# Token sums by matrix multiply, or by VectorE's block transposes: the RMS root of a fused attention and gated-MLP kernel

## The chip, the cores and the metric

One NeuronCore of a Trainium2 chip runs the whole program. The metric is the device time of one launch in microseconds (us), the median of several runs. A profile of one execution of the kernel before gives the span from the first to the last instruction and every instruction's start and length.

## The reference

Windowed attention over 8 batches, 8 heads, 576 positions of 64 numbers (four heads see the last 32 positions, four heads every fourth of the last 128) makes x, 4608 tokens of 512 numbers. Then comes a gated MLP with an RMS norm in front:

```python
rms = np.sqrt(np.mean(x * x, axis=-1, keepdims=True) + 1e-06)
xn = x / rms * rms_g
g = xn @ w_gate                               # 512 -> 1536
silu = g * (1.0 / (1.0 + np.exp(-g)))
out = (silu * (xn @ w_val)) @ w_out           # 1536 -> 512
```

Everything is float32. What matters here is the row `rms`: for each token, a sum of 512 squares, and then its inverse root multiplied into all 512 numbers.

## The kernel before

**Tiling.** The tokens are cut into 16 units of 288 (`u` = 0 to 15, half a batch each). Inside a unit the features lie on the 128 partitions in four blocks (`c` = 0 to 3), and the 288 tokens are the columns. The MLP's 1536 inner features are 12 blocks of 128 (`j` = 0 to 11). From u = 1 on, a float32 product is made of three matmuls on rounded parts (high by high, high by low, low by high), written `hi` and `lo` in names.

**Ticks.** The program is one list of ticks written out in advance. For each j of a unit there are three: `gate` (12 matmuls into `g`), `val` (12 into `v`) and `proj` of the j before (12 into the four `acc` banks). So a unit's MLP has 36 ticks. The attention of unit u + 1 is threaded between them: one burst at a time makes scores `s`, transposes `t` and outputs `o`. I number a unit's norm by the ticks of the MLP of the unit before it: tick 28 is a `val`, 29 a `proj`, 30 a `gate`, 31 a `val`, and tick 36 is the first `gate` that reads the normed x.

**Order in a tick.** `later(dt, rank, fn)` puts a piece of work off by dt ticks. `flush` issues a tick's pieces sorted by rank, ahead of the tick's matmuls. Each engine runs what it is given in that order and never lets a later instruction pass an earlier one that waits. Ranks that matter: the row sums and scaling of attention (`scores_norm`) -1, `prod` and `tanh` 0, the split of h into high part (ScalarE, `hhi`) and low part (GpSimd, `hlo`) 0.5, `silu` 0.6, `scores_max` 0.7, the low part of q (`q_lo`) 0.9 in tick 29.

**PSUM.** There are eight banks and each tag has one. `g` of block j and `v` of block j + 1 share a bank, `v` of j and `g` of j + 1 the other one. In a `val` tick in which attention also transposes, the tile `t` is taken new from the bank of that j's `g` (`bank("g", j)`), so its first write comes after the last reader of that `g`, which is `silu` (L724). Tick 31 is such a tick in the norms of u = 3 to 14; u = 15 has no next unit and so no attention then.

**The norm before**, for u = 1 to 15. `square` (ScalarE) squares each block of x and the squares are added into `xsq`, the last addition on VectorE in tick 28. `rms_sum` ends tick 28 with three matmuls of float32 (six in the trace) that sum over the partitions. `rms_root` in tick 29: VectorE adds the epsilon (L593), GpSimd raises [96, 3] numbers to the power -0.5 (L594), splits them (L599, L600); VectorE and ScalarE put both parts on diagonals (L608, L612). `rms_apply` ends tick 30 with two matmuls against ones (L628), which leave the root of every token on all partitions in the PSUM tile `bps`. `normal` (L642) multiplies x by it in ticks 31, 32, 32 and 33, and `part` splits the result for the MLP of tick 36 on.

Of the kernel before, what the change touches and what calls it, by code (L numbers as in the profile page):

```python
# [77 lines left out]
def attn_moe(ctx: ExitStack, tc: tile.TileContext, qk_in, v_in, w_gate, w_val, w_out, rms_g, outT):  # L78
# [16 lines left out]
    A.copy(out=ones, in_=one.to_broadcast([P, P]))  # L95
    inv = cst.tile([P, 2], F32, name="inv")
    G.memset(inv, 1.0 / DM)
    mhalf = cst.tile([QB, U // QB], F32, name="mhalf")
    G.memset(mhalf, -0.5)
    mask = cst.tile([QB, P], F32, name="mask")  # L100
    G.memset(mask, 0.0)
# [18 lines left out]
    def later(dt, rank, fn):  # L120
        put_off.setdefault(now[0] + dt, []).append((rank, fn))
# [299 lines left out]
    def take(u, c, i, o, heads_of=(0, 1)):  # L421

        blocks, nq, _ = geometry(u, c)
        if (u, c) not in xraw:
            xraw[u, c] = sb.tile([P, U], F32, tag="xraw", name=f"xraw_{u}_{c}", bufs=NC)
        x = xraw[u, c]
        if c < NC // 2:
            to = x[:, QB * i:QB * i + nq]
        else:
            to = x.rearrange("p (j r) -> p r j", r=DIL)[:, i, :]  # L430
        if u == 0:
            A.copy(out=to, in_=o[:, :nq])
        elif u < NEX:
            for a in range(2):
                A.copy(out=to[a * D:(a + 1) * D], in_=o[a * D:(a + 1) * D, a * nq:(a + 1) * nq])
        else:
            for a in heads_of:
                ours, cols = to[a * D:(a + 1) * D], 2 * a * nq
                V.tensor_reduce(out=ours, in_=o[:D, cols:cols + 2 * nq].rearrange("d (t q) -> d q t", t=2),  # L439
                                axis=mybir.AxisListType.X, op=ALU.add)  # L440
                V.tensor_tensor(out=ours, in0=o[D:, cols:cols + nq], in1=ours, op=ALU.add)  # L441
        if i == len(blocks) - 1 and 1 in heads_of:
            if u == 0 and c == NC - 1:
                square(u, c)
                return
            dt = 1 if c != 1 or u < NEX else 4
            later(dt, 0.44 if u >= NEX and (now[0] + dt - ends) % 3 == 0 else 2.5 if u else 1.9, lambda: square(u, c))

    def square(u, c):
        first = c == 0  # L450
        sq = sb.tile([P, U], F32, tag="xsq" if first else "tmp", name=f"sq_{u}_{c}", bufs=1 if first else 2)
        x = xraw[u, c]
        A.activation(out=sq, in_=x, func=AF.Square)
        if u == 0:
            if c < NC - 1:
                G.tensor_scalar(out=x, in0=x, scalar1=gs[:, c:c + 1], scalar2=1.0, op0=ALU.mult, op1=ALU.mult)
            else:
                A.activation(out=x, in_=x, func=AF.Copy, scale=gs[:, c:c + 1])
        if u == 0:
            squares.append(sq)  # L460
        elif first:
            xsq[u] = sq
        else:
            later(1, 0.4, lambda: (V if c == NC - 1 or u == 1 else G).tensor_tensor(out=xsq[u], in0=xsq[u], in1=sq, op=ALU.add))

    def bursts(u):
        return [(u, c, i) for c in range(NC) for i in range(len(geometry(u, c)[0]))]
# [16 lines left out]
    def products(q, t, o, t_ps, s_tag="s", o_tag="o", wait=0):  # L484
# [50 lines left out]
        if o:  # L535
            if o[0] < NEX or wait:
                later(1, 0.41 if o[0] < NEX else 0.55, lambda: take(*o, o_ps))
            else:
                for a in range(2):
                    later(1, (0.1, 0.3)[a], lambda a=a: take(*o, o_ps, (a,)))  # L540
            if o[0] < NEX:
                later(1, 9, lambda: load_v(further(o, 3)))
            far = further(o, 2)
            if far and far[0] >= NEX:
                split_v(far, 8 if o[0] < NEX else 1)
# [30 lines left out]
    def rms_sum(u):  # L576
        if u == 0:
            part_sum(NC - 1)
            later(1, -1.2, lambda: rms_root(u, sum_ps))
            later(1, 0.75, spread_first)  # L580
            return
        r_ps = ps.tile([QB, NB, 2], F32, tag="o", name=f"rps_{u}")
        for i in range(NB):
            PE.matmul(r_ps[:, i, :], xsq[u][:, i * QB:(i + 1) * QB], inv, start=True, stop=True)
        later(1, 0.1 if u == 1 else -1.2, lambda: rms_root(u, r_ps))

    def rms_root(u, r_ps):
        r = sb.tile([QB, NB], F32, tag="rst", name=f"rst_{u}", bufs=2)
        total = r_ps[:, :, 0]
        if u == 0:  # L590
            V.tensor_reduce(out=r, in_=r_ps[..., 0].rearrange("q c i -> q i c"), axis=mybir.AxisListType.X, op=ALU.add)
            total = r
        V.tensor_scalar(out=r, in0=total, scalar1=1e-6, scalar2=None, op0=ALU.add)  # L593
        G.tensor_tensor(out=r, in0=r, in1=mhalf, op=ALU.pow)  # L594
        if u == 0:
            rst[u] = [r]
            return
        r_hi, r_lo = (sb.tile([QB, NB], F32R, tag=f"rst_{p}", name=f"rst_{p}_{u}", bufs=1) for p in ("hi", "lo"))
        G.tensor_copy(out=r_hi, in_=r)  # L599
        G.tensor_tensor(out=r_lo, in0=r, in1=r_hi, op=ALU.subtract)  # L600
        rst[u] = []

        def spread():
            for p in (r_hi, r_lo):
                d = sb.tile([QB, NB, QB], F32R, tag="tmp", name=f"rd_{u}_{len(rst[u])}", bufs=2)
                rst[u].append(d)
                if p is r_hi:
                    V.tensor_tensor(out=d, in0=ident[:QB, None, :QB].to_broadcast([QB, NB, QB]),  # L608
                                    in1=p[:, :, None].bitcast(F32).to_broadcast([QB, NB, QB]), op=ALU.mult)
                    continue  # L610
                for i in range(NB):
                    A.activation(out=d[:, i, :], in_=ident, func=AF.Copy, scale=p[:, i:i + 1].bitcast(F32))  # L612
        later(1, 0.1, spread)
# [8 lines left out]
    root, spare = [], []  # L622

    def rms_apply(u):
        ds = rst.pop(u)
        b_ps = ps.tile([P, U], F32, tag="o", name=f"bps_{u}")
        for k, d in enumerate(ds):
            PE.matmul(b_ps, (ones if u else ones32)[:QB, :], d.rearrange("p i q -> p (i q)"),  # L628
                      start=k == 0, stop=k == len(ds) - 1)
        xs[u] = {}  # L630
        if u == 0:
            root.append(sb.tile([P, U], F32, tag="tmp", name="root", bufs=2))
            later(2, 0.66, lambda: A.copy(out=root[0], in_=b_ps))

        def normal(c):
            x = xraw[u, c]
            if u == 0:
                xn = sb.tile([P, U], F32, tag="xhi", name=f"xn_{c}", bufs=4)
                V.tensor_tensor(out=xn, in0=x, in1=b_ps, op=ALU.mult)
                xs[u][c] = xn  # L640
                return
            V.scalar_tensor_tensor(out=x, in0=x, scalar=gs[:, c:c + 1], in1=b_ps,  # L642
                                   op0=ALU.mult, op1=ALU.mult)

        def part(c):
            x = xraw.pop((u, c))
            k = (u * NC + c) % 6
            if u > 1 and not spare:
                spare.append(cst.tile([P, 3, U], F32R, tag=f"slot{state['free']}", name="spare"))
            if k == 5 and u > 1:  # L650
                hi = spare[0][:, 2]
            else:
                pool, tag, bufs = (sb, "xhi", 4) if k < 4 else (late[0], ("xhi", "ot")[k - 4], 1)
                hi = pool.tile([P, U], F32R, tag=tag, name=f"xhi_{u}_{c}", bufs=bufs)
            if c < 2 and u % 2 == 0:
                lo = spare[0][:, c]
            else:
                lo = late[0].tile([P, U], F32R, tag=f"xlo{c // 2}", name=f"xlo_{u}_{c}", bufs=2)
            A.copy(out=hi, in_=x)
            (V if c % 2 else G).tensor_tensor(out=lo, in0=x, in1=hi, op=ALU.subtract)  # L660
            xs[u][c] = (hi, lo)

        for c in range(NC):
            later((1, 2, 2, 3)[c] if u else 1, 0.6 + (0.03 * (c > 1) if u == 0 else 0), lambda c=c: normal(c))
            if u:
                later((2, 3, 4, 5)[c], 0.45 if c == NC - 1 and u > 1 else 0.6, lambda c=c: part(c))
# [100 lines left out]
    def give(u, d):  # L767
        pool, tag, bufs = ((sb, "xsq", 1) if u == 0 else (late[0], "ot", 1), (sb, "hhi", 2), (sb, "tmp", 2), (sb, "tmp", 2))[d]
        o = pool.tile([P, U], F32, tag=tag, name=f"ot_{u}_{d}", bufs=bufs)
        if (u, d) == (NU - 1, NC - 1):  # L770
            V.tensor_scalar(out=o[:, U // 2:], in0=acc[u, d][:, U // 2:], scalar1=0.5, scalar2=None, op0=ALU.mult)
            A.activation(out=o[:, :U // 2], in_=acc[u, d][:, :U // 2], func=AF.Copy, scale=0.5)
        elif d % 2:
            V.tensor_scalar(out=o, in0=acc[u, d], scalar1=0.5, scalar2=None, op0=ALU.mult)
        else:
            A.activation(out=o, in_=acc[u, d], func=AF.Copy, scale=0.5)
# [180 lines left out]
```

## Time and profile before

| | us |
|---|---|
| median of 3 runs | 1104.48 |
| lowest and highest run | 1103.78, 1105.72 |
| span of the profiled execution, first to last instruction | 1102.2 |
| TensorE busy in it | 1095.2 (99%) |
| VectorE busy | 782.7 (71%) |
| GpSimd busy | 670.1 (61%) |
| ScalarE busy | 614.8 (56%) |

The profiled execution has no separate launch time: its span is 2.3 us below the median of the runs, which is the part of a launch outside the span. The granted TensorE clock is at its full 2.4 GHz over the span. A matmul of 288 columns is listed at about 0.29 us, but its neighbours start about 0.13 us apart, since they overlap; what a matmul costs is the step from its start to the next one's.

### The profile page before, as it was taken

What the parts mean: (1) busy time and instruction counts of PE and PEld (TensorE: products, weight loads), DVE (VectorE), ACT (ScalarE), POOL (GpSimd) and SP (SyncE); (2) the same over time, 40 slices, a digit from 0 to 9 for tenths busy, and PEclk for the clock granted to TensorE, in tenths of its full rate; (3) what the DMA queues carried; (4) which work ended last, traced back from release to release, by engine and by line L of the source; (5) the groups of instructions that cost most, each with busy time, mean ns of one, the idle gap of its engine ahead of it and who ended that gap; (6) DMA issues with size and microseconds to landing.
All of it is one profiled execution on the core that took longest, in us unless ns stands there. A gap on an engine that the chain in (4) does not pass through costs nothing.

```text
span 1102.2 us, 25627 instructions
## 1 busy us (share of the span) xinstructions
PE 1095.2 (99%) x8416; PEld 1071.6 (97%) x8416; DVE 782.7 (71%) x3094; ACT 614.8 (56%) x2202; POOL 670.1 (61%) x1152
## 2 busy tenths in 40 slices
PE   8999999999999999999999999999999999999998
PEld 7787999999999999999999999999999999999998
DVE  7988667868687676867768677686867768687412
ACT  6895676556465564646556464664646556464211
POOL 6333589657585675757657575775758657584211
PEclk9999999999999999999999999999999999999999
DMA  9774213212131131312212131131212212120000
GB/s 255 205 263 163 79 51 87 74 35 82 43 94 52 41 97 30 95 42 73 66 36 85 43 94 43 50 96 37 79 43 83 64 32 83 53 74 13 18 6 22
DMA packets 61543, 82.18 MB, mean 75 GB/s; under 512 B 7298, under 2 KB 41090, under 8 KB 61410
## 3 DMA queue, kind: packets, MB, share of 16 engines
q1 hardware_dynamic: 61410, 80.54, 24.3%
q8 instruction: 67, 1.10, 0.4%
q14 instruction: 66, 0.54, 0.2%
HBM read 71.08 MB, written 9.44 MB: 73 GB/s over the span
## 4 chain that ended last, share of the span: by engine, by line
PE 95%; POOL 2%; DVE 1%; ACT 1%; issue 1%; POOLq 0%; ACTq 0%; DVEq 0%
PE acc L682 17%; PE g L682 17%; PE v L682 17%; PE acc L679 9%; PE g L679 9%; PE v L679 9%; PE o L512 3%; PE s L524 3%; PE acc L676 2%; PE v L676 2%; PE g L676 2%; PE t L497 2%; PE s L521 1%; PE g L497 1%; PE busy L802 1%; PE o L509 1%
## 5 line engine op out<-in xcount | busy, mean ns | idle before, releaser
L749 POOL TENSOR_TENSOR hlo<-th,hhi 128x288 fp32r<-128x288 f32 x179 | 145.2, 811 | 161.3 <-ACT hhi L748 147.8
L401 ACT ACTIVATE t<-t,sum 96x128 f32<-96x128 f32 (+3 forms) x448 | 165.9, 374 | 107.8 <-DVE sum L386 105.1
L682 PE MATMUL acc<-hhi,lo 128*128 128x288 f32 x720 | 212.7, 295 | 0.0
L417 POOL TENSOR_SCALAR t<-t,sum 96x128 f32<-96x128 f32 (+3 forms) x416 | 147.6, 366 | 88.4 <-DVE sum L411 74.6
L719 ACT ACTIVATE th<-g 128x288 f32<-128x288 f32 x180 | 73.8, 410 | 195.2 <-PE g L682 100.5
L682 PE MATMUL g<-xhi,lo 128*128 128x288 f32 x612 | 180.3, 295 | 0.0
L682 PE MATMUL v<-xhi,lo 128*128 128x288 f32 x612 | 180.2, 294 | 0.0
L439 DVE TENSOR_REDUCE xraw<-o 64x72 f32<-64x144 f32 (+1 forms) x364 | 117.1, 322 | 84.0 <-PE o L512 79.5
L724 DVE SCALAR_TENSOR_TENSOR th<-th,g 128x288 f32<-128x288 f32 x180 | 80.8, 449 | 102.0 <-ACT th L719 78.4
L682 PEld LDWEIGHTS acc<-hhi,lo 128*128 128x128 f32 x720 | 135.4, 188 | 0.0
L324 POOL TENSOR_TENSOR vhl<-vt,vhl 128x128 fp32r<-128x128 f32 x182 | 84.4, 464 | 70.4 <-ACT vhl L320 66.8
L748 ACT CAST hhi<-th 128x288 fp32r<-128x288 f32 x180 | 77.7, 432 | 75.5 <-DVE th L737 74.6
L682 PEld LDWEIGHTS g<-xhi,lo 128*128 128x128 f32 x612 | 115.2, 188 | 0.0
L682 PEld LDWEIGHTS v<-xhi,lo 128*128 128x128 f32 x612 | 115.1, 188 | 0.0
L737 DVE TENSOR_TENSOR th<-th,v 128x288 f32<-128x288 f32 x180 | 79.8, 444 | 43.6 <-PE v L682 43.5
L441 DVE TENSOR_TENSOR xraw<-o,xraw 64x72 f32<-64x72 f32 (+1 forms) x364 | 101.1, 278 | 12.5
L679 PE MATMUL acc<-hhi,hi_o 128*128 128x288 f32 x360 | 109.0, 303 | 0.0
L679 PE MATMUL g<-xhi,hi_g 128*128 128x288 f32 x357 | 107.0, 300 | 0.0
L682 PE MATMUL acc<-hlo,hi_o 128*128 128x288 f32 x360 | 106.4, 296 | 0.0
L363 POOL TENSOR_TENSOR qs<-qk,qs 64x288 fp32r<-64x288 f32 x104 | 84.3, 811 | 24.1 <-ACT qs L358 16.9
L354 POOL TENSOR_TENSOR ks<-qk,ks 128x288 fp32r<-128x288 f32 (+2 forms) x104 | 96.8, 936 | 3.1
L682 PE MATMUL g<-xlo,hi_g 128*128 128x288 f32 x322 | 95.1, 295 | 0.0
(193 smaller groups left out, 3458.6 us busy)
## 6 DMA issues: line engine op xcount, KB each, us to landing
qk<-in_qk_dram SPq DMA_DIRECT2D x60, 288.0 KB, 2.9
vt<-in_v_dram SPq DMA_DIRECT2D x196, 64.0 KB, 1.9
qk<-in_qk_dram SPq DMA_DIRECT2D x30, 352.0 KB, 2.9
out_dram<-ot SPq DMA_DIRECT2D x64, 144.0 KB, 1.9
qk<-in_qk_dram SPq DMA_DIRECT2D x30, 304.0 KB, 2.9
raw<-in_w_gate_dram SPq DMA_DIRECT2D x12, 512.0 KB, 4.6
raw<-in_w_val_dram SPq DMA_DIRECT2D x12, 512.0 KB, 3.3
raw<-in_w_out_dram SPq DMA_DIRECT2D x12, 512.0 KB, 4.2
```

Source lines behind the costliest of these rows:

```text
L324: G.tensor_tensor(out=vp[:, :, 1], in0=vs.pop(b), in1=vp[:, :, 0], op=ALU.subtract)
L354: ek.tensor_tensor(out=ks[:, 1, :nkt], in0=kr, in1=ks[:, 0, :nkt], op=ALU.subtract)
L363: eq.tensor_tensor(out=qs[D:], in0=qr[D:], in1=qs[D:], op=ALU.subtract)
L401: A.activation(out=t[:nq, a, :n], in_=t[:nq, a, :n], func=AF.Exp, scale=-1.0, bias=sm[:nq, a, 0:1], accum_out=None if by_rows(u, c, i) els ...
L417: (V if u == 0 and (c, i) > (NC - 1, 1) else G).tensor_scalar(out=t[:nq, a, :n], in0=t[:nq, a, :n], scalar1=sm[:nq, a, 3:4], scalar2=1.0, ...
L439: V.tensor_reduce(out=ours, in_=o[:D, cols:cols + 2 * nq].rearrange("d (t q) -> d q t", t=2), axis=mybir.AxisListType.X, op=ALU.add)
L441: V.tensor_tensor(out=ours, in0=o[D:, cols:cols + nq], in1=ours, op=ALU.add)
L679: PE.matmul(out, wh[:, cc, :], xh, start=start, stop=False)
L682: PE.matmul(out, w[:, cc, :], v, start=False, stop=stop and k == 1)
L724: V.scalar_tensor_tensor(out=t, in0=t, scalar=1.0, in1=g, op0=ALU.add, op1=ALU.mult)
L737: V.tensor_tensor(out=t, in0=t, in1=v_ps[:, :U], op=ALU.mult)
L749: (V if (u, j) == (NU - 1, NJ - 1) else G).tensor_tensor(out=lo, in0=t, in1=hi, op=ALU.subtract)
```

## The change

For u = 2 to 15 the two groups of matmuls go (u = 0 and 1 keep them). `fold`, from tick 27, sums with VectorE's transpose, which turns each 32 x 32 block by itself: `xsq` is turned, each row of 32 numbers is added up, and the sums stand on four groups of 32 partitions, nine columns each.

- Tick 26: the last `square`, one tick earlier than before (rank 8). Tick 27: its addition, the transpose [128, 288] and the reduction to [128, 9], all on VectorE.
- Tick 28: `gather`, three ScalarE copies of [32, 9] onto partitions 0 to 31 (rank 0.65); `mean`, two VectorE instructions (rank 0.9).
- Tick 29: `root_of`, the power on GpSimd over [32, 9], rank 0.6, so behind `hlo` with 0.5. Before, the power over [96, 3] had rank -1.2 and stood ahead of it.
- Tick 30: `scatter`, two ScalarE copies, 32 partitions onto the next 32, and those 64 onto the other 64 (rank 0.7); `spread`, a VectorE transpose of each number held for 32 columns, into [128, 288] in SBUF (rank 0.9).
- `normal` stays where it was and reads that SBUF tile in place of `bps`.

For u = 2 `gather` and `mean` come in tick 27, the power in 28, the rest in 29. At the very end, the last output block is scaled by one ScalarE instruction of 288 columns and not by one half on VectorE and one on ScalarE.

```diff
+            if c == NC - 1 and u >= NEX:
+                return
             dt = 1 if c != 1 or u < NEX else 4
...
+            if c == NC - 1 and u >= NNAT:
+                later(1, 0.9, lambda: fold(u))
...
+            if o[0] >= NEX and o[1:] == (NC - 1, len(geometry(*o[:2])[0]) - 1):
+                later(1, 8, lambda: square(*o[:2]))
...
+        if u >= NNAT:
+            return
         r_ps = ps.tile([QB, NB, 2], F32, tag="o", name=f"rps_{u}")
...
+    def fold(u):
+        nt = U // 32
+        dt = 1 if u >= NEX else 0
+        turned = sb.tile([P, U], F32, tag="tmp", name=f"sqt_{u}", bufs=2)
+        V.transpose(out=turned, in_=xsq[u])
+        r = sb.tile([P, 4, nt], F32, tag="rst", name=f"rst_{u}", bufs=1)
+        V.tensor_reduce(out=r[:, 0], in_=turned.rearrange("p (b j) -> p b j", j=32), axis=mybir.AxisListType.X, op=ALU.add)
+        g = sb.tile([P, nt], F32, tag="rroot", name=f"rroot_{u}", bufs=1)
+
+        def gather():
+            for k in range(1, 4):
+                A.copy(out=r[:32, k], in_=r[32 * k:32 * (k + 1), 0])
+
+        def mean():
+            V.tensor_reduce(out=g[:32], in_=r[:32].rearrange("p k b -> p b k"), axis=mybir.AxisListType.X, op=ALU.add)
+            V.tensor_scalar(out=g[:32], in0=g[:32], scalar1=1.0 / DM, scalar2=1e-6, op0=ALU.mult, op1=ALU.add)
+
+        def root_of():
+            G.tensor_tensor(out=g[:32], in0=g[:32], in1=mhalf[:32], op=ALU.pow)
+
+        def scatter():
+            for n in (32, 64):
+                A.copy(out=g[n:2 * n], in_=g[:n])
+
+        def spread():
+            rst[u] = sb.tile([P, U], F32, tag="tmp", name=f"root_{u}", bufs=2)
+            V.transpose(out=rst[u].rearrange("p (b j) -> p b j", j=32), in_=g[:, :, None].to_broadcast([P, nt, 32]))
+
+        if dt:
+            later(1, 0.65, gather)
+            later(1, 0.9, mean)
+        else:
+            gather()
+            mean()
+        later(1 + dt, 0.6, root_of)
+        later(2 + dt, 0.7, scatter)
+        later(2 + dt, 0.9, spread)
...
     def rms_apply(u):
-        ds = rst.pop(u)
-        b_ps = ps.tile([P, U], F32, tag="o", name=f"bps_{u}")
-        for k, d in enumerate(ds):
-            PE.matmul(b_ps, (ones if u else ones32)[:QB, :], d.rearrange("p i q -> p (i q)"),
-                      start=k == 0, stop=k == len(ds) - 1)
+        b_ps = rst.pop(u)
+        if u < NNAT:
+            ds, b_ps = b_ps, ps.tile([P, U], F32, tag="o", name=f"bps_{u}")
...
-        if (u, d) == (NU - 1, NC - 1):
-            V.tensor_scalar(out=o[:, U // 2:], in0=acc[u, d][:, U // 2:], scalar1=0.5, scalar2=None, op0=ALU.mult)
-            A.activation(out=o[:, :U // 2], in_=acc[u, d][:, :U // 2], func=AF.Copy, scale=0.5)
-        elif d % 2:
+        if d % 2 and (u, d) != (NU - 1, NC - 1):
             V.tensor_scalar(out=o, in0=acc[u, d], scalar1=0.5, scalar2=None, op0=ALU.mult)
```

## Rows read from the trace of the kernel before

**Rows 1.** The page, first part: busy us, share of the span, instructions.
```profile
PE 1095.2 (99%) x8416; PEld 1071.6 (97%) x8416; DVE 782.7 (71%) x3094; ACT 614.8 (56%) x2202; POOL 670.1 (61%) x1152
```

**Rows 2.** Chain of waits, TensorE only: us in total, times, longest; first and last.
```profile
PE busy L802 <- ACT ones L95: 2.4, 1, 2.4
...
PE bps L628 <- ACT rd L612: 0.2, 1, 0.2
```

**Rows 3.** Timeline, TensorE, norm of u = 7: start us, us, instruction, how many.
```profile
500.98 0.59 PE L584 MATMUL rps<-inv,sq 128*96 128x2 f32 x6
501.43 0.38 PE L679 MATMUL acc<-hhi,hi_o 128*128 128x288 f32 x1
501.65 0.30 PE L682 MATMUL acc<-hlo,hi_o 128*128 128x288 f32 x1
...
504.93 0.43 PE L628 MATMUL bps<-rd,ones 96*128 96x288 f32 x2
505.20 0.29 PE L679 MATMUL v<-xhi,hi_o 128*128 128x288 f32 x1
...
506.79 0.33 PE L497 MATMUL t<-ident,t 96*96 96x96 f32 x2
```

**Rows 4.** The same, norm of u = 2.
```profile
174.83 0.29 PE L628 MATMUL bps<-rd,ones 96*128 96x288 f32 x1
...
175.56 0.30 PE L679 MATMUL v<-xhi,hi_o 128*128 128x288 f32 x1
```

**Rows 5.** Timeline, VectorE, norm of u = 7; in brackets idle before it and the releaser.
```profile
499.32 0.46 DVE L464 TENSOR_TENSOR sq<-sq,sq 128x288 f32<-128x288 f32 x1 [1.05 <-ACT sq L453]
...
501.61 0.16 DVE L593 TENSOR_SCALAR rst<-rps 96x3 f32<-96x3 f32 x1
501.69 0.14 DVE L410 TENSOR_REDUCE sum<-sum 96x2 f32<-96x4 f32 x1
501.87 0.16 DVE L411 RECIPROCAL sum<-sum 96x2 f32<-96x2 f32 x1
501.95 0.43 DVE L737 TENSOR_TENSOR th<-th,v 128x288 f32<-128x288 f32 x1
...
505.63 0.46 DVE L724 SCALAR_TENSOR_TENSOR th<-th,g 128x288 f32<-128x288 f32 x1 [0.86 <-ACT th L719]
```

**Rows 6.** Timeline, ScalarE, the same stretch.
```profile
501.74 0.19 ACT L401 ACTIVATION_READ_ACCUMULATOR t<-t,sum 96x1 f32 x1
...
502.41 0.43 ACT L748 CAST hhi<-th 128x288 fp32r<-128x288 f32 x1
503.54 0.91 ACT L612 ACTIVATE rd<-ident,rst_lo 96x96 fp32r<-96x96 f32 x3 [0.69 <-POOL rst_lo L600]
505.19 0.41 ACT L719 ACTIVATE th<-g 128x288 f32<-128x288 f32 x1 [0.75 <-PE g L682]
```

**Rows 7.** Timeline, GpSimd, the same stretch.
```profile
501.85 0.86 POOL L594 TENSOR_TENSOR rst<-rst,mhalf 96x3 f32<-96x3 f32 x1
502.77 0.18 POOL L599 CAST rst_hi<-rst 96x3 fp32r<-96x3 f32 x1
503.04 0.46 POOL L600 TENSOR_TENSOR rst_lo<-rst,rst_hi 96x3 fp32r<-96x3 f32 x1
503.49 0.66 POOL L417 TENSOR_SCALAR t<-t,sum 96x96 f32<-96x96 f32 x2
504.12 0.80 POOL L749 TENSOR_TENSOR hlo<-th,hhi 128x288 fp32r<-128x288 f32 x1
505.00 0.81 POOL L363 TENSOR_TENSOR qs<-qk,qs 64x288 fp32r<-64x288 f32 x1
```

**Rows 8.** Timeline, all engines, the end of the span.
```profile
1098.44 0.41 ACT L776 ACTIVATE ot<-acc 128x288 f32<-128x288 f32 x1 [0.39 <-PE acc L682]
1098.84 0.31 DVE L771 TENSOR_SCALAR ot<-acc 128x144 f32<-128x144 f32 x1 [0.34 <-PE acc L682]
1099.18 0.29 ACT L772 ACTIVATE ot<-acc 128x144 f32<-128x144 f32 x1 [0.33 <-DVE ot L771]
```

More of the change, by code (lines that the diff above doesn't have):

```diff
@@ L97, in attn_moe @@
     G.memset(inv, 1.0 / DM)
-    mhalf = cst.tile([QB, U // QB], F32, name="mhalf")
+    mhalf = cst.tile([QB, U // 32], F32, name="mhalf")
     G.memset(mhalf, -0.5)
@@ L585, in rms_sum @@
         later(1, 0.1 if u == 1 else -1.2, lambda: rms_root(u, r_ps))
+    def fold(u):
[29 more added lines that the diff above has]
+        later(2 + dt, 0.9, spread)
     def rms_root(u, r_ps):
-        r = sb.tile([QB, NB], F32, tag="rst", name=f"rst_{u}", bufs=2)
+        r = sb.tile([QB, NB], F32, tag="rst", name=f"rst_{u}", bufs=1)
         total = r_ps[:, :, 0]
@@ L593, in rms_root @@
         V.tensor_scalar(out=r, in0=total, scalar1=1e-6, scalar2=None, op0=ALU.add)
-        G.tensor_tensor(out=r, in0=r, in1=mhalf, op=ALU.pow)
+        G.tensor_tensor(out=r, in0=r, in1=mhalf[:, :NB], op=ALU.pow)
         if u == 0:
@@ L624, in rms_apply @@
     def rms_apply(u):
-        ds = rst.pop(u)
-        b_ps = ps.tile([P, U], F32, tag="o", name=f"bps_{u}")
-        for k, d in enumerate(ds):
-            PE.matmul(b_ps, (ones if u else ones32)[:QB, :], d.rearrange("p i q -> p (i q)"),
-                      start=k == 0, stop=k == len(ds) - 1)
+        b_ps = rst.pop(u)
+        if u < NNAT:
+            ds, b_ps = b_ps, ps.tile([P, U], F32, tag="o", name=f"bps_{u}")
+            for k, d in enumerate(ds):
+                PE.matmul(b_ps, (ones if u else ones32)[:QB, :], d.rearrange("p i q -> p (i q)"),
+                          start=k == 0, stop=k == len(ds) - 1)
         xs[u] = {}
```

## Prediction, made before the result

> **What bounds the kernel now.** I read the page's busy times first: TensorE is busy for 1095.2 of 1102.2 us, the others for 56 to 71% [rows 1]. Busy there includes overlap, so I looked next at who makes TensorE wait. The chain of waits has little for it: 2.4 us at the start, then waits of some tenths, the shortest a 0.2 [rows 2]. So nearly every nanosecond taken from TensorE's stream shortens the run, and every new wait of TensorE lengthens it. The third view is the timeline of one norm, engine by engine; the norms of u = 3 to 14 repeat it within about 0.1 us, so I work with u = 7 and count twelve like it.
>
> **What goes from TensorE.** A normal step from matmul to matmul: the `val` of tick 31 starts at 505.20 and its twelve are over when `t` starts at 506.79, 0.13 us each. The sums hold the stream from 500.98 to 501.43, and the next matmul starts 0.22 and not 0.13 later: 0.53 us together. The spread holds it from 504.93 to 505.20: 0.27 us [rows 3]. Together 0.80 us, for u = 3 to 15: 13 x 0.80 = 10.4 us. In u = 2 the spread holds it from 174.83 to 175.56, since the second matmul waits: 0.73 us [rows 4], with the same 0.53: 1.3 us. **Gain: 11.7 us.**
>
> **The tail.** Before, the two halves run one after the other, the first starting at 1098.84 and the second ending at 1099.18 + 0.29 = 1099.47. One instruction of 288 columns takes 0.41, so 1099.25 [rows 8]: **gain 0.2 us.** All told 11.9 us, if nothing new waits.
>
> **What is added, and what covers it.** *Tick 27, VectorE.* Neither a block transpose nor this reduction is in the trace. Bounds from VectorE's rows: 0.14 (two columns) and 0.46 (288 columns with two inputs) [rows 5]; both new ones pass over 288 columns, so I take 0.43 each, 0.9 us. The addition only moves, and leaves its own 0.46 with the 1.05 idle before it [rows 5]: 1.5 us of cover, so nothing is late. Were both instructions twice that, 0.2 us would pass on to `silu` of tick 28. *Tick 26 and 28, ScalarE.* The square moves; three small copies come, between 0.19 (one column) and 0.30 each (a third of the 0.91) [rows 6], 0.7 us at the most, and three of 0.30 go. The mean's inputs are there before VectorE reaches `mean`. *Tick 28, VectorE.* `mean` stands where the epsilon's addition stood, at 501.61. That one held the next for 0.08, and a dependent pair of small ones runs at 0.18 and 0.08 from start to start [rows 5]: 0.26 for 0.08. So `prod` of tick 29 starts at about 502.13 in place of 501.95, and `hhi` ends at 502.84 + 0.18 = 503.02 [rows 6]. Bounds: 0.1 and 0.3 us late.
>
> *Tick 29, GpSimd.* Here is the doubtful price. The queue becomes: the two scalings L417 (0.66, ready before `hhi`), `hlo` (0.80, from 503.04 on), the power, `q_lo` (0.81). The power starts at 503.04 + 0.80 + 0.07 = 503.91; before, it started at 501.85 [rows 7]. Its length over [32, 9] stands nowhere. Below: 0.86, the row over [96, 3] unchanged, since both hold 288 numbers. Above: three times that, 2.59. Between them: copying and subtracting [96, 3] take 0.18 and 0.46, so what is the power's own is 0.68 or 0.40 for three columns. If that grows with the columns, nine cost 0.18 + 2.04 = 2.22 or 0.46 + 1.20 = 1.66 [rows 7]. I take the middle, **1.95 us**, so it ends at 505.86. A price by columns is the nearer one, because copy and power have the same shape and differ by a factor of five, which a fixed cost of starting an instruction doesn't explain.
>
> The Trainium skill, "GPSIMD Engine Reference", sections Specifications and Instruction dispatch, says that each of eight cores owns 16 partitions and runs a software loop over its share, and that the instruction is done when all are. By that rule 32 partitions leave six cores without data and nine columns make the loop three times as long; it speaks for the price by columns and so against this change, where a flat price would leave a gain of about 5 us. No row of before has a second width of the power to test it on.
>
> *Tick 30.* `scatter` is two copies on ScalarE, the second dependent: 0.04 after the power (as L612 starts 0.04 after L600 ends), then 2 x 0.24 between the bounds above, to 506.38. On VectorE `spread` waits for it: 506.43 to 506.86 with 0.43.
>
> **What waits behind those two.** ScalarE keeps its order: `tanh` of tick 31 stands behind `scatter`. It waits for `g`, whose matmuls end 0.53 earlier now, and could start at 505.19 - 0.53 = 504.66; it starts at 506.38 and ends at 506.79 [rows 6]. On VectorE the sums and reciprocal of tick 31 (0.18 + 0.08) stand behind `spread`, then comes `silu` (0.46): 506.86 + 0.26 = 507.12 to 507.58, where it ended at 506.09 [rows 5]. And `silu` is the last reader of the bank into which `t` of tick 31 is written. TensorE comes to `t` at 506.79 - 0.80 = 505.99 [rows 3]. With 0.07 for the hand-over it waits until 507.65: **1.66 us in each of twelve norms, 19.9 us.** As a formula the wait is the power's length less 0.29. The same lateness reaches TensorE a second way: `q_lo` now ends at 505.86 + 0.08 + 0.81 = 506.75, and the score matmuls right behind `t` read it; that wait lies inside the first. The transfer that `q_lo` issues on SP's queue comes about 0.9 us later than the 505.81 of before [rows 7]; what it loads is read in ticks 32 and 33, which are as late themselves, so nothing more.
>
> Behind `silu`, `normal` and `prod` follow while TensorE does the `t`, the scores and the twelve matmuls of tick 32, so the bank for tick 33 is free again. In u = 15 there is no `t`; `prod` of tick 32 is read a tick later and TensorE waits 0.1 us or not at all. In u = 2 all steps come a tick sooner: nothing.
>
> **The sum.** 1102.2 - 11.9 + 19.9 + 0.1 = 1110.3 us of span. The profiled span lies 2.3 us under the median of the runs, which I keep: **1112.6 us**, 8 us slower.
>
> **Rivals.**
> *The power costs about what it did* (0.86 to 1.1). For it: [96, 3] and [32, 9] hold the same 288 numbers, and the rows show one width alone. Against it: the 0.18 of the copy. Then it ends at 504.77, the wait is 0.57 x 12 = 6.8, and the time is 1104.5 - 11.9 + 6.8 = 1099.4. This is the case on the other side; it decides for faster as soon as the power is under 0.29 + 11.9 / 12 = 1.28 us.
> *The stall doesn't come*, and the change gives what it takes from TensorE: 1104.5 - 11.9 = 1092.6. That needs the power done by 504.2, so 0.3 us long, or `prod` and `hhi` much earlier than I have them. For it speaks only that TensorE waits nowhere now [rows 2].
> *The two cancel*: a power of 1.1 to 1.5 gives waits of 9.7 to 14.5 us, and 1102.3 to 1107.1.
> *It is longer still*: three times 0.86 gives a wait of 2.30 x 12 = 27.6, and 1120.2.
>
> **Chances.** A power by columns, 1.5 to 2.6 us: 0.60, of which 0.06 above 2.5. Cancelling: 0.12. A flat power: 0.18. No stall: 0.10. By 0.2%, 2.2 us, which is about what a measurement can tell here from no change: slower 0.60, same 0.12, faster 0.28. The likeliest case's own range, with the power between 1.66 and 2.22, is 1109 to 1116 us. For 8 in 10 the range takes in the flat power at 1099 and nearly all of the power by columns: 1098 to 1119 us.
>
> **What would show it.** The line of the power over [32, 9], with its mean: about 1.95 us (1.28 decides). In the chain of waits a new row, TensorE at `t` (L497) waiting for VectorE's `th` (L724), twelve times about 1.7 us; in the timeline ScalarE's scatter idle until GpSimd's power ends, `tanh` right behind it, `spread` before `silu`. No `rps`, and `bps` only for u = 0 and 1; TensorE's busy time 10 to 12 us lower outside those waits. The forecast is wrong if the power is short, if `hlo` and the power start much before 503.9, or if `t` doesn't need the bank that `silu` reads. If the waits stand at the scores and not at `t`, `q_lo` set the end, and the sum would be some 0.9 us a norm smaller.

## The result and the profile after

| | before | after |
|---|---|---|
| median, us | 1104.38 (8 runs) | 1118.03 (8 runs) |
| lowest run | 1103.75 | 1117.08 |
| span of the profiled execution | 1102.2 | 1117.9 |
| ratio of after to before | | 1.0115 (95% interval 1.0089 to 1.0141) |

The change makes the kernel slower: the medians differ by 13.7 us, or 1.24%, and the ratio with its interval puts it at 1.15% (0.89 to 1.41%). The forecast was 8 us slower with a range to 1119. One of the eight runs before took 1116.10 us, and the other seven lie between 1103.75 and 1105.90.

The spans differ by 15.7 and not by 13.7, because the profiled execution of after is a long one (1119.63 us). Its granted clock is 0.56 from 32 to 34 us and 0.59 from 34 to 36, a mean of full speed and of the half level (1.2 of 2.4 GHz), after four microseconds in which TensorE was listed as busy throughout; before has 1.00 there. That costs 1.4 us, and another 0.65 arises in the first 10 us, a part that varies from 0 to 0.8 us between the traces. Six of the runs below have the same stretch at half clock, one of them the kernel before with nothing but a wider constant, so it does not come with the change.

The busy times, which answer to [rows 1], and the first and the last row of TensorE's chain of waits with its two new ones, which answer to [rows 2]:

```profile
PE 1095.8 (98%) x8304; PEld 1066.2 (95%) x8304; DVE 820.4 (73%) x3135; ACT 618.8 (55%) x2230; POOL 681.6 (61%) x1124
```

```profile
PE t L501 <- DVE th L771: 13.3, 19, 1.0
PE busy L846 <- ACT ones L95: 2.4, 1, 2.4
PE s L528 <- DVE sum L410: 1.6, 2, 0.9
...
PE t L501 <- DVE sum L410: 0.2, 1, 0.2
```

TensorE has 112 instructions fewer, and its listed busy time is no shorter; its idle time grows from 7.0 to 22.1 us. The new first row is the one that the forecast named: `t` waits for `silu` (L771). There are 19 such waits, though, not twelve. VectorE is busy 37.7 us longer; the five new instructions of a norm (L599, L601, L609, L610 and L621 below) make 14 x 1.79 = 25.1 of that, even before what they replace is taken off.

The norm of u = 7 after, GpSimd first, against [rows 7]:

```profile
510.61 0.66 POOL L417 TENSOR_SCALAR t<-t,sum 96x96 f32<-96x96 f32 x2 [0.56 <-DVE sum L411]
511.41 0.81 POOL L796 TENSOR_TENSOR hlo<-th,hhi 128x288 fp32r<-128x288 f32 x1
512.17 1.80 POOL L613 TENSOR_TENSOR rroot<-rroot,mhalf 32x9 f32<-32x9 f32 x1
514.05 0.80 POOL L363 TENSOR_TENSOR qs<-qk,qs 64x288 fp32r<-64x288 f32 x1
```

ScalarE, against [rows 6], and VectorE, against [rows 5], cut to what is new or late:

```profile
508.73 0.61 ACT L606 COPY rst<-rst 32x9 f32<-32x9 f32 x3 [0.21 <-DVE rst L601]
...
510.89 0.43 ACT L795 CAST hhi<-th 128x288 fp32r<-128x288 f32 x1 [0.26 <-DVE th L784]
514.01 0.43 ACT L617 COPY rroot<-rroot 32x9 f32<-32x9 f32 x2 [2.68 <-POOL rroot L613]
514.46 0.41 ACT L766 ACTIVATE th<-g 128x288 f32<-128x288 f32 x1
```

```profile
507.73 0.48 DVE L599 STREAM_TRANSPOSE sqt<-sq 128x288 f32<-128x288 f32 x1
508.24 0.46 DVE L601 TENSOR_REDUCE rst<-sqt 128x9 f32<-128x288 f32 x1
...
509.85 0.21 DVE L609 TENSOR_REDUCE rroot<-rst 32x9 f32<-32x36 f32 x1
510.09 0.16 DVE L610 TENSOR_SCALAR rroot<-rroot 32x9 f32<-32x9 f32 x1
...
510.43 0.43 DVE L784 TENSOR_TENSOR th<-th,v 128x288 f32<-128x288 f32 x1
...
514.53 0.48 DVE L621 STREAM_TRANSPOSE root<-rroot 128x288 f32<-128x288 f32 x1 [1.92 <-POOL rroot L613]
514.93 0.11 DVE L410 TENSOR_REDUCE sum<-sum 96x2 f32<-96x4 f32 x1
515.07 0.17 DVE L411 RECIPROCAL sum<-sum 96x2 f32<-96x2 f32 x1
515.16 0.43 DVE L771 SCALAR_TENSOR_TENSOR th<-th,g 128x288 f32<-128x288 f32 x1
```

TensorE, against [rows 3]: tick 29's first two matmuls, the last of those ahead of `t`, and `t` of tick 31.

```profile
509.61 0.30 PE L726 MATMUL acc<-hhi,hi_o 128*128 128x288 f32 x1
509.75 0.30 PE L729 MATMUL acc<-hlo,hi_o 128*128 128x288 f32 x1
...
514.50 0.29 PE L729 MATMUL v<-xhi,lo 128*128 128x288 f32 x1
515.73 0.34 PE L501 MATMUL t<-ident,t 96*96 96x96 f32 x2 [0.94 <-DVE th L771]
```

Read from GpSimd across: the power ends at 513.97, `scatter` starts 0.04 later, `tanh` stands right behind it, `spread` starts when the scatter has passed and stands ahead of `silu`, and `t` starts 0.14 after `silu`'s listed 515.59. TensorE has no matmul to start for 1.23 us, 1.10 more than a step. That is the predicted chain link by link; over the twelve norms the delay is 1.05 to 1.22 us.

Setting the start of every group of TensorE's matmuls in after against the same group in before gives the ledger of the profiled execution (us):

| | predicted | measured |
|---|---|---|
| sums and spread gone, u = 3 to 15 | -10.4 | -10.2 (0.44 + 0.08 + 0.26 each) |
| the same in u = 2 | -1.3 | -1.1 |
| wait at `t` of tick 31, twelve norms | +19.9 | +14.1 (1.05 to 1.22 at `t`, a few hundredths behind it) |
| a second delay, from the `val` of tick 37 to the scores behind its `t`, in u = 4, 6, 8, 10, 12, 14 | 0 | +4.3 (0.7 each) |
| new delays in u = 2 | 0 | +3.7 |
| step from matmul to matmul, 132.55 to 133.04 ns | 0 | +3.2 (0.49 ns x 15 units x 432) |
| half clock near 34 us | 0 | +1.4 |
| first 10 us | 0 | +0.65 |
| tail and rest | -0.1 | -0.3 |
| together | +8.1 | +15.7 |

In the first row, 0.44 is what the first matmul of `acc` gains, 0.08 shows at the group behind `acc`, because the second matmul of `acc` follows the first by 0.14 us and no longer by 0.22 [rows 3], and 0.26 is the spread.

The step is the mean distance between the starts of successive matmuls inside the groups `g`, `v` and `acc`, after the first 200 us and without distances over 200 ns, some 5,500 of them in a trace; in every stretch of 100 us that of after is the longer one, by 0.3 to 0.7 ns.

Three of these rows (the second delay, u = 2 and the step) have no place in the forecast; the clock and the first 10 us belong to this execution. What `normal` does now gives the first hint for the second delay and for u = 2. All its instructions in after, then those of u = 8 beside the work of GpSimd at the same time, and the wait that follows some 7 us later:

```profile
L689 DVE SCALAR_TENSOR_TENSOR xraw<-xraw,gs,root x56: 504/544/2669, 179.1 to 1051.8; 128x288 f32<-128x288 f32 x56
L689 DVE SCALAR_TENSOR_TENSOR xraw<-xraw,gs,bps x4: 503/507/509, 105.0 to 109.5; 128x288 f32<-128x288 f32 x4
```

```profile
585.37 2.04 DVE L689 SCALAR_TENSOR_TENSOR xraw<-xraw,gs,root 128x288 f32<-128x288 f32 x1
587.34 0.44 DVE L771 SCALAR_TENSOR_TENSOR th<-th,g 128x288 f32<-128x288 f32 x1
...
589.72 1.12 DVE L707 TENSOR_TENSOR xlo<-xraw,spare 128x288 fp32r<-128x288 f32 x1 [0.18 <-ACT spare L706]
```

```profile
585.10 0.94 POOL L417 TENSOR_SCALAR t<-t,sum 96x128 f32<-96x128 f32 x2
586.01 1.09 POOL L354 TENSOR_TENSOR ks<-qk,ks 128x416 fp32r<-128x416 f32 x1
```

```profile
594.13 0.38 PE L501 MATMUL t<-ident,t 96*128 96x96 f32 x2 [0.24 <-DVE th L771]
```

The three numbers behind a group are its shortest, median and longest instruction in ns. Where `normal` reads the root from PSUM (`bps`, u = 1) it takes 507 and never more than 509; where it reads it from SBUF (`root`) the same instruction takes up to 2669. The long ones lie beside GpSimd's instructions: of the 56 that read `root`, the 14 with no instruction of GpSimd beside them take 504 to 514 ns, though ScalarE works beside most of these too, and all 16 above 600 ns have GpSimd at work for 0.6 us or more of their time. Work of GpSimd beside it is not enough by itself, since others with 0.3 us of it keep 505.

### The profile page after: what moved, and what is told of

It reads as the page before. It is cut to its first block, busy times and chain, and to the rows that moved or that the text cites. A ratio compares the mean times of both kernels' runs of the same rounds, so it can differ in the third digit from the quotient of the medians.

```text
span 1117.9 us, 25444 instructions
## 1 busy us (share of the span) xinstructions
PE 1095.8 (98%) x8304; PEld 1066.2 (95%) x8304; DVE 820.4 (73%) x3135; ACT 618.8 (55%) x2230; POOL 681.6 (61%) x1124
## 4 chain that ended last, share of the span: by engine, by line
PE 76%; DVE 14%; POOL 3%; issue 3%; ACT 3%; DMA 0%; ACTq 0%; DVEq 0%; POOLq 0%
PE acc L729 13%; PE g L729 13%; PE v L729 13%; PE acc L726 7%; PE g L726 7%; PE v L726 7%; PE o L516 3%; POOL rroot L613 2%; PE s L528 2%; PE acc L723 2%; PE t L501 2%; PE v L723 2%; PE g L723 2%; DVE t L386 2%; DVE t L381 1%
## 5 line engine op out<-in xcount | busy, mean ns | idle before, releaser
L417 POOL TENSOR_SCALAR t<-t,sum 96x128 f32<-96x128 f32 (+3 forms) x416 | 151.9, 377 | 104.4 <-DVE sum L411 90.9
L771 DVE SCALAR_TENSOR_TENSOR th<-th,g 128x288 f32<-128x288 f32 x180 | 80.3, 446 | 68.5 <-ACT th L766 56.5
L363 POOL TENSOR_TENSOR qs<-qk,qs 64x288 fp32r<-64x288 f32 x104 | 84.1, 809 | 19.1 <-ACT qs L358 11.9
```

What stands on the lines that cost most here:

```text
L363: eq.tensor_tensor(out=qs[D:], in0=qr[D:], in1=qs[D:], op=ALU.subtract)
L417: (V if u == 0 and (c, i) > (NC - 1, 1) else G).tensor_scalar(out=t[:nq, a, :n], in0=t[:nq, a, :n], scalar1=sm[:nq, a, 3:4], scalar2=1.0, ...
L771: V.scalar_tensor_tensor(out=t, in0=t, scalar=1.0, in1=g, op0=ALU.add, op1=ALU.mult)
```

## The experiments

Three theories went into the runs. **A**: the power behind `hlo` is late, and since `scatter` and `spread` stand ahead of `tanh` and `silu` in their queues, `t` waits. **B**: `normal` reads two tensors from SBUF now, is slow beside GpSimd's work, and that makes the second delays. **C**: the constant of exponents `mhalf`, widened from three to nine columns for the new power, moves other tiles in SBUF, and the step lengthens. Its rival throughout: the step comes with the changed work. All ratios are to the kernel before, run on the same chip (medians 1104.0 to 1104.4). The changed kernel's 1118.03 is from the result alone, so a difference to it goes across chips and is good to a few tenths.

### Theory A: the power ahead, and no power at all

The first run is the changed kernel with the power's rank back ahead of `hlo`.

```diff
-        later(1 + dt, 0.6, root_of)
+        later(1 + dt, -1.2, root_of)
```

> Theory A (the late power): transposes of tick 31 wait for silu, silu and tanh stand behind scatter and spread, and these wait for a power of 1.8 us that begins behind hlo. With the power at rank -1.2, ahead of the scalings and of hlo, it begins about 1.5 us earlier, the twelve waits of TensorE at tick 31 fall from about 1.1 us each to under 0.3, and the time falls by about 10 us to 1108. Theory B (two SBUF inputs): normal reads the root and x both from SBUF and takes 1 to 2.7 us in place of 0.5 beside GpSimd's work, which makes a later silu late; this stays, some 4 us. If A is wrong, the waits at tick 31 stay and the time is 1117 to 1118.

Measured 1103.75 us, ratio 0.9997 (0.9988 to 1.0006): 14.3 us below the changed kernel, more than the 10 that were expected. In TensorE's waits, those at `t` of tick 31 are gone and six short ones and one of u = 2 are left:

```profile
PE s L528 <- DVE sum L410: 2.2, 1, 2.2
PE t L501 <- DVE th L771: 1.3, 6, 0.2
```

The power still takes 1.80 us. So it is its place and not its length alone that costs, and the six waits of the even units are another matter.

The second run takes the power's duration away, by a multiplication in its place; the root is left out of the result.

```diff
-            G.tensor_tensor(out=g[:32], in0=g[:32], in1=mhalf[:32], op=ALU.pow)
+            G.tensor_tensor(out=g[:32], in0=g[:32], in1=mhalf[:32], op=ALU.mult)
```

> The power is replaced by a multiplication of the same shape, so the root is left out of the result. Theory A: the instruction takes about 0.2 us, the waits of tick 31 vanish, and the time falls by 12 to 13 us to about 1105; what stays above 1092.6 is then theory B's and the norm of u = 2. If the waits at tick 31 come from something else (the later q_lo, the longer queue of VectorE), they stay at a time over 1112.

Measured 1101.32 us, ratio 0.9974 (0.9963 to 0.9986). Even without any power the kernel gains 3 us and not the 11.9 of the forecast's "no stall". The rest is given back elsewhere: the second delays stand as they were (4.3 us, of which the profile lists six waits of 1.4), u = 2 is 1.1 us late, and the step stays at 133.04 ns.

### Theory A against its rival: the order in two queues

`q_lo` is behind the power too, and the score matmuls behind `t` need it. This run leaves the power late and puts `scatter` behind `tanh` and `spread` and `normal` behind `silu`, in tick 31. `room` takes the root's tile in tick 30, as before.

```diff
-        later(2 + dt, 0.7, scatter)
-        later(2 + dt, 0.9, spread)
+        later(2 + dt, 0.9, room)
+        later(3 + dt, 0.05, scatter)
+        later(3 + dt, 0.61, spread)
...
-            later((1, 2, 2, 3)[c] if u else 1, 0.6 + (0.03 * (c > 1) if u == 0 else 0), lambda c=c: normal(c))
+            later((1, 2, 2, 3)[c] if u else 1, 0.6 + (0.03 * (c > 1) if u == 0 else 0.02 if u >= NNAT else 0), lambda c=c: normal(c))
```

> The change, with scatter put behind tanh of tick 31 and spread behind silu of tick 31 (normal of tick 31 behind both); the power stays behind hlo. Theory A, order in the queues: tanh and silu no longer stand behind the power, the twelve waits at tick 31 fall from 1.1 us to under 0.3, and the time falls by 9 to 12 us to 1106 to 1109. Rival: the scores right behind those transposes wait for the low part of q, which still stands behind the power on GpSimd; then TensorE keeps waiting some 0.3 to 0.6 us in each of the twelve, and the time is 1110 to 1114. Theory B's waits stay in both.

Measured 1108.18 us, ratio 1.0036 (1.0023 to 1.0049), 9.9 us below the changed kernel. GpSimd and ScalarE in u = 7 of this run:

```profile
508.65 1.80 POOL L613 TENSOR_TENSOR rroot<-rroot,mhalf 32x9 f32<-32x9 f32 x1
510.52 0.81 POOL L363 TENSOR_TENSOR qs<-qk,qs 64x288 fp32r<-64x288 f32 x1
```

```profile
509.78 0.41 ACT L770 ACTIVATE th<-g 128x288 f32<-128x288 f32 x1 [1.97 <-PE g L733]
510.48 0.43 ACT L617 COPY rroot<-rroot 32x9 f32<-32x9 f32 x2 [0.29 <-POOL rroot L613]
```

`q_lo` starts as late as in the changed kernel, 0.07 after the power, but `tanh` no longer waits for the power, and the delays of tick 31 fall to 0.07 to 0.17 us, 1.1 in all and not 14.1. The order in the queues of ScalarE and VectorE makes the wait; the late `q_lo` does not. The run gains 9.9 us and not 13: around ticks 34 to 37, behind the later `normal`, 4.4 us of delay come anew.

### Theory B: where the root lies

First from the kernel before: its spread's result is copied from PSUM to SBUF by ScalarE, and `normal` reads the copy. Nothing else changes.

```diff
+        if u >= NNAT:
+            flat = sb.tile([P, U], F32, tag="tmp", name=f"flat_{u}", bufs=2)
+            later(1, 0.05, lambda: A.copy(out=flat, in_=b_ps))
+        else:
+            flat = b_ps
...
-            V.scalar_tensor_tensor(out=x, in0=x, scalar=gs[:, c:c + 1], in1=b_ps,
+            V.scalar_tensor_tensor(out=x, in0=x, scalar=gs[:, c:c + 1], in1=flat,
```

> The kernel before with one thing added: ScalarE copies the spread root from PSUM into SBUF, and normal reads it there. Theory B: the last normal of a norm takes 1 to 2 us in place of 0.5, TensorE waits in every second norm, and the time rises by 2 to 4 us to 1106 to 1108. If two SBUF inputs cost nothing by themselves and only the late power made those waits, normal stays near 0.5 us and the time at 1104 to 1105. Theory A says nothing of this run: no wait at tick 31 in either case.

Measured 1109.28 us, ratio 1.0048 (1.0033 to 1.0063). Against before, TensorE loses 1.2 us in u = 2 and 0.7 in each of u = 4, 6, ..., 14, at the same `val` and `t` as in the changed kernel; everything else together comes to less than 0.2 us. `normal` in this run:

```profile
L647 DVE SCALAR_TENSOR_TENSOR xraw<-xraw,gs,flat x56: 509/514/2035, 176.6 to 1041.2; 128x288 f32<-128x288 f32 x56
```

Then from the changed kernel: `spread` writes its tile in PSUM.

```diff
-            rst[u] = sb.tile([P, U], F32, tag="tmp", name=f"root_{u}", bufs=2)
+            rst[u] = ps.tile([P, U], F32, tag="o", name=f"root_{u}")
```

> The change with one thing different: spread writes its transpose into the PSUM bank that the matmuls used, and normal reads it there. Theory B: every normal is back at 0.5 us, the second group of waits (every second norm, about 0.7 us each, and 1 us in u = 2) goes, and the time falls by 4 to 6 us to 1112 to 1114. Theory A: the twelve waits of tick 31 stay at about 1.1 us each. If B is wrong, the time stays at 1117 to 1118.

Measured 1112.08 us, ratio 1.0077 (1.0061 to 1.0092), 6.0 us below the changed kernel. `normal` and TensorE's first wait:

```profile
L689 DVE SCALAR_TENSOR_TENSOR xraw<-xraw,gs,root x56: 490/504/509, 179.1 to 1045.1; 128x288 f32<-128x288 f32 x56
```

```profile
PE t L501 <- DVE th L771: 12.2, 12, 1.1
```

Twelve waits are left of 19, those of tick 31; the second delays are gone. The two runs meet at 5 to 6 us: an SBUF root costs 5.2 put into the kernel before, more than the 2 to 4 that were expected, and gives 6.0 back taken out of the changed one. The Trainium skill, "GPSIMD Engine Reference", section Specifications, says that GpSimd shares its SBUF interfaces with VectorE, with contention for VectorE's instructions that have two SBUF inputs. The rows agree: with one input in PSUM, the 42 of `normal` that have GpSimd's work beside them take 501 to 509 ns, like those without, and with both in SBUF up to 2035 and 2669. No run took GpSimd's work away; in the traces it is the instructions without it that stay short.

### Theory C: the step from matmul to matmul

The kernel before with the wide constant alone:

```diff
-    mhalf = cst.tile([QB, U // QB], F32, name="mhalf")
+    mhalf = cst.tile([QB, U // 32], F32, name="mhalf")
```

> Theory C (addresses): in every kernel with the change TensorE's step from matmul to matmul inside a group is 133.04 ns on the mean, in the kernel before and in its copy with the root in SBUF 132.55; over some 7000 such steps that is 3.4 us. The change makes the constant of -0.5 wider, 36 bytes a partition for 12, and all the tiles allocated behind it, the weights too, move by 32 bytes. This run is the kernel before with that tile widened and nothing else. C: the step goes to about 133.0 ns and the time up by 3 to 4 us, to 1107 to 1108. If the slower step has another cause (what VectorE or GpSimd do meanwhile), the step stays at 132.55 and the time at 1104 to 1105. Theories A and B say nothing of this run.

Measured 1105.13 us, ratio 1.0007 (0.9998 to 1.0016), step 132.59 ns. **Theory C as put is refuted.** But in this kernel all later tiles move by the same 32 bytes; in the changed one, which has other small tiles as well, the weights move by 32 and the streamed tiles by 128 and 192, multiples of 64 (by the addresses in the built kernels). So the theory was put anew: what counts is where the weights start in a partition against the tiles that stream past them. Two runs test it from both sides. The changed kernel with the constant at three columns again, read as a broadcast column, and five roots' rows in place of four as padding (the power of u = 0 and 1 then reads the constant as it is):

```diff
-    mhalf = cst.tile([QB, U // 32], F32, name="mhalf")
+    mhalf = cst.tile([QB, U // QB], F32, name="mhalf")
...
-        r = sb.tile([P, 4, nt], F32, tag="rst", name=f"rst_{u}", bufs=1)
+        r = sb.tile([P, 5, nt], F32, tag="rst", name=f"rst_{u}", bufs=1)[:, :4]
...
-            G.tensor_tensor(out=g[:32], in0=g[:32], in1=mhalf[:32], op=ALU.pow)
+            G.tensor_tensor(out=g[:32], in0=g[:32], in1=mhalf[:32, :1].to_broadcast([32, nt]), op=ALU.pow)
```

> The changed kernel with its constant of exponents back at one element a row (read as a broadcast column) and the five roots' tile padded, so that only the first pool, which holds the weights, lies 32 bytes further back, as in the kernel before; every wait stays. Theory C' (the step from matmul to matmul hangs on where the weights lie in SBUF against the tiles that stream past them): the step inside the long groups goes from 133.04 ns back to about 132.5, over some 7000 steps 3.4 us, so 1114 to 1115 us, ratio about 1.009. Rival (the step comes with the changed work itself, the new transposes and copies): the step stays at 133.0 and the time at 1118.

And the kernel before with the wide constant and one buffer less of a small tile behind the weights, so that the weights move and the streamed tiles stay:

```diff
-        r = sb.tile([QB, NB], F32, tag="rst", name=f"rst_{u}", bufs=2)
+        r = sb.tile([QB, NB], F32, tag="rst", name=f"rst_{u}", bufs=1)
```

> The kernel before with the wide constant and one buffer less of a root's tile, so that the weights lie 32 bytes further and the streamed tiles where they lay; nothing else differs in its work. Theory C': the step goes from 132.55 ns to about 133.0, 3 us and more over the kernel: 1107 to 1108 us, ratio about 1.003. Rival (the step does not hang on addresses, or only on those that an earlier run moved together): 132.5 ns and 1104 to 1105 us, ratio within 0.001 of 1.

Start of the tiles in their partition, in bytes modulo 64, with the step. A quarter of the low x parts and a sixth of the high ones lie in the tile `spare`, which moves with the weights; "x and h parts" are the others.

| kernel | weights | x and h parts | step, ns |
|---|---|---|---|
| before | 32 | 32 | 132.55 |
| wide constant alone | 0 | 0 | 132.59 |
| changed, narrow constant | 32 | 32 | 132.44 |
| all three edits (below) | 32 | 32 | 132.45 |
| changed | 0 | 32 | 133.04 |
| before, weights shifted | 0 | 32 | 132.95 |

The narrow constant gives 1114.52 us, ratio 1.0093 (1.0079 to 1.0106), 3.5 below the changed kernel, with the 19 waits as they were (14.0 us). The shifted weights give 1106.54, ratio 1.0022 (1.0013 to 1.0032), 2.5 above before, with no new wait; 0.40 ns x 6,480 steps are 2.6. The first lies in its expected range and the second half a microsecond under it, with the steps that the theory in its new form had, and the step does not come with the changed work. Both runs also move the tiles of x ahead of its splitting, of `th` and of most of q along with the weights, so it is not shown that the weights' offset and not that of these tiles is what counts. Nor is it shown why an offset matters.

### The price of the power by its width

The prediction's doubtful price, measured by itself: the changed kernel with fourteen more powers at its end, each of a partition count and a width, so its time (1129.27 us) says nothing.

```diff
+    trial = late[0].tile([P, U], F32, tag="xlo0", name="trial", bufs=2)
+    G.memset(trial, 0.5)
+    col = 0
+    for parts, wide in ((96, 3), (32, 9), (32, 3), (96, 9), (32, 1), (32, 6), (96, 6)) * 2:
+        G.tensor_tensor(out=trial[:parts, col:col + wide], in0=trial[:parts, 200:200 + wide],
+                        in1=mhalf[:parts, :1].to_broadcast([parts, wide]) if wide > 9 else mhalf[:parts, :wide], op=ALU.pow)
+        col += wide
```

> The change with fourteen powers more on GpSimd behind the last work of that engine, in seven shapes, each twice: 96 and 32 partitions by 3, 6 and 9 columns, and 32 by 1; nothing reads them. If the price goes by columns, 32 and 96 partitions take the same, 3 columns 0.86 us, 9 columns 1.80, so 0.155 us a column and 0.4 fixed: 6 columns 1.33 and 1 column 0.55. If it goes by numbers in all, [32, 3] takes a third of the own part of [96, 3] and [96, 9] three times that of [32, 9]. The run itself ends some 10 us later, since these powers do.

The groups of GpSimd in that stretch (busy us, mean ns of one, idle before):

```profile
L937 POOL TENSOR_TENSOR trial<-trial,mhalf 96x9 f32<-96x9 f32 x2 | 3.6, 1786 | 0.0
L937 POOL TENSOR_TENSOR trial<-trial,mhalf 32x9 f32<-32x9 f32 x2 | 3.6, 1786 | 0.0
L937 POOL TENSOR_TENSOR trial<-trial,mhalf 32x6 f32<-32x6 f32 x2 | 2.6, 1322 | 0.0
...
L937 POOL TENSOR_TENSOR trial<-trial,mhalf 96x3 f32<-96x3 f32 x2 | 1.7, 854 | 0.1
L937 POOL TENSOR_TENSOR trial<-trial,mhalf 32x3 f32<-32x3 f32 x2 | 1.7, 841 | 0.0
L937 POOL TENSOR_TENSOR trial<-trial,mhalf 32x1 f32<-32x1 f32 x2 | 1.1, 542 | 0.0
```

From one column to nine it is (1786 - 542) / 8 = 156 ns a column on 387 ns, and 96 partitions cost what 32 do. That agrees with what the forecast drew from the Trainium skill, "GPSIMD Engine Reference", sections Specifications and Instruction dispatch: the price goes by columns, and partitions left out save nothing.

### All three edits together, and unit two

The power ahead, the root in PSUM and the narrow constant with its padding are put together, each as above.

> The change with three things different: the power at rank -1.2, the spread into PSUM, and the constant as wide as before and read as one broadcast column (a tile beside is padded so that only the first pool's addresses differ from the change's). If A, B and C are separate and add up: 1118 less 14 (as measured for the power ahead) less 6 (as measured for PSUM) less 3.4 for a step back at 132.55 ns, so 1094 to 1096, which would be faster than both kernels. Without C 1097 to 1099, with a step of 133.0.

Measured 1094.73 us, ratio 0.9915 (0.9902 to 0.9929), 23.3 us below the changed kernel; one by one they gave 14.3, 6.0 and 3.5, which is 23.8. TensorE's waits are back to the start's 2.4 us, one of 0.7 and some tenths:

```profile
PE busy L846 <- ACT ones L95: 2.4, 1, 2.4
PE s L528 <- DVE sum L410: 0.7, 1, 0.7
```

The 0.7 belongs to u = 2, whose norm is done in one go. The last run steps it over four ticks like the others, with its last square a tick earlier:

```diff
-            if c == NC - 1 and u >= NEX:
+            if c == NC - 1 and u >= NNAT:
...
-            if o[0] >= NEX and o[1:] == (NC - 1, len(geometry(*o[:2])[0]) - 1):
+            if o[0] >= NNAT and o[1:] == (NC - 1, len(geometry(*o[:2])[0]) - 1):
...
-        dt = 1 if u >= NEX else 0
+        dt = 1
```

> The fastest kernel so far (power ahead, root spread into PSUM, narrow constant: 1094.73 us) with unit two's norm stepped over four ticks like the later ones, in place of that norm's short form in one go. Theory: unit two's norm still keeps the scores' matmuls waiting for the sum of squares (0.7 us) and is about a microsecond late after it; stepped, both go: 1093 us, ratio about 0.990. Rival: the tick it is moved into is as full, and the time stays at 1094.7 or rises by up to 1 us.

Measured 1093.48 us, ratio 0.9902 (0.9889 to 0.9916). The wait falls to 0.4 and the span from 1092.0 to 1091.5; the medians differ by 1.25, but the two intervals overlap, so half a microsecond is what the traces show and no more is claimed. This version is 10.5 us faster than the kernel before on the same chip and 24.6 than the changed one.

## Why the prediction was right, and where its sum was not

The forecast, slower by way of the power, came true, with 1118.03 inside the range, 1 us from its end, 5.4 us above the value and above the 1109 to 1116 of the likeliest case. That the sum came this close was in part luck: a wait oversized by 5.8 us covered for half of three terms that the forecast did not have, 11.2 us together.

**The gain.** 0.78 us a norm for u = 3 to 15, where 0.80 was forecast: 10.2 and 10.4 us. The sign that went with it, TensorE's busy time 10 to 12 us lower, did not come. A matmul is listed for about 0.29 us where its step is 0.13, so part of a delay is listed as busy: of 22 us of delays only 15.1 show as idle time, and the other 7 with the longer step's 3.2 take up most of the gain. The tail gave nothing that shows: from the start of the last matmul to the end of the span it is 1102.2 - 1098.50 = 3.7 us before and 1117.9 - 1114.12 = 3.8 after.

**The power.** 1.80 us, where 1.95 was taken and 1.66 to 2.22 was the range by columns. The width trial shows that it goes by columns, as the copy beside it suggested.

**The power's start.** The forecast had it 2.93 us after the tick's first matmul; it starts 512.17 - 509.61 = 2.56 after it. `prod` is the cause: I had it 0.18 us later than before, behind `mean`, and forgot that what held it before, L593's wait for the sums' matmuls, goes with them. After, `prod` starts 510.43 - 509.61 = 0.82 after the tick's start, before it was 501.95 - 500.98 = 0.97 [rows 3, 5] and the forecast had 1.15.

**The wait.** These two make 0.37 + 0.15 = 0.52 us of the difference; the predicted 1.66 becomes 1.14, and 1.05 to 1.22 was measured. The term was mis-sized, 14.1 for 19.9 us, the mechanism was right: removed by the power's place (14.3 us) and, with the power as late as ever, by the order of `scatter` and `tanh` (9.9 us). The bound "under 1.28 us decides for faster" fell with the terms that were missing: they take 11.2 us, about the whole gain of 11.3, and the run without any power gained 3 us only.

**`normal` "stays where it was".** This is the step that failed. The line stays and its operand moves from PSUM to SBUF, and I gave that no price. It costs 5 to 6 us by two runs, u = 2 included: there two blocks of `normal` take 1.95 and 2.67 us, and the scores behind them wait 0.9 us. "Nothing" for u = 2 was wrong with it, and also for 1.1 us of delay, 0.7 of it the scores' wait for VectorE, that stay when the root lies in PSUM.

**The addresses.** The change also widens the constant of exponents from three columns to nine, a line that the excerpt of the diff ahead of the prediction leaves out and that the first run of theory C makes by itself. No view of before can price it: 3.5 us by the run that takes it back.

## What to carry to other kernels

When work leaves a saturated engine, follow every queue in which its replacement stands ahead of something that engine waits for: here the same power, ahead of `hlo` and not behind it, was worth 14.3 us, more than the 11.3 that the change took from TensorE. Look at where an operand moves, PSUM or SBUF, as closely as at what is computed: writing the new root to PSUM and not to SBUF was one line and gave 6.0 us. And when a trace shows every matmul a little slower, compare tile offsets before looking for a cause in the work.

## What the runs showed of the hardware

- GpSimd's power takes 387 ns and 156 ns a column, on 32 partitions as on 96 (1786 ns for both at nine columns).
- VectorE's `normal`, a scalar_tensor_tensor of 128x288, with two SBUF inputs took 0.50 to 2.67 us, the long ones beside GpSimd's work, and 0.50 to 0.51 where GpSimd did nothing beside it; with one input in PSUM it took 0.49 to 0.51 throughout.
- VectorE's 32x32 transpose of 128x288 float32 takes 478 ns.
- With weights and streamed tiles at the same offset modulo 64 bytes the step between matmuls of 288 columns is 132.4 to 132.6 ns, and 132.95 to 133.04 with 32 bytes between them, in the six kernels of the table; other tiles moved along with the weights, and the cause is open.
